# 44 instead of 70 small zero products at the start, a planner whose engines begin later, halved first units and new ranks in an attention and channel-mixing kernel

## The chip, the cores and the metric

The kernel runs on one core of one Trainium2 chip. The metric is the time of one execution on the device in microseconds (us); less is better. A profile is one execution taken by the hardware profiler. Engines are written as in the profile: PE is TensorE's matmul stream and PEld its weight loads, DVE is VectorE, ACT is ScalarE, POOL is GpSimd, SP is SyncE, whose queue starts the DMA transfers.

## What is computed

Three layers follow each other, on a batch of 4 with 576 positions. In the reference, shortened:

```python
# attention: 8 heads of 64; heads 0-3 look back 32 positions, heads 4-7 look back 32 steps of 4
scores = np.where(mask, 1/np.sqrt(64) * q @ k.T, -1e9)
x = softmax(scores) @ v                    # heads joined: (4, 576, 512)
# mixing with the position before
xk = mu_k * x + (1 - mu_k) * x_prev;  xr = mu_r * x + (1 - mu_r) * x_prev
y = sigmoid(xr @ w_r) * (np.maximum(xk @ w_k, 0)**2 @ w_v)
# low rank token mixing and a channel MLP
u = y + ((y.T @ U) @ V).T
out = u + np.maximum(u @ w_ch1, 0) @ w_ch2
```

Weights and activations are kept as float32, and most products run as three matmuls of a high and a low part. The big weights arrive as 64-bit words that DVE and ACT put together into float32 in the kernel.

## The kernel before

**Staging.** The 2304 positions are eight chunks of 288. Attention runs in *units* (one pair of heads, one part of one batch entry): the first four units one by one (`attend`), all later ones two at a time (`attend2`). A unit is: scores on PE (40 small matmuls, L850), masked and negated scores with their least value on DVE (`low`, L775), exponentials with their sums on ACT (`exp`, L784), the reciprocal of the sums (`inv`, L789 and L790), a scaling (`norm`, L801), transposes on PE (L881), a copy from PSUM on ACT (L497), the product with v on PE (L893), and a copy into x. After that come d (the difference to the position before, POOL) and the two mixtures xr, xk (DVE, L1022).

Chunk 0 of the second layer runs in plain float32: first the four rows of w_r (L1081), then eight rows of w_k and eight of w_v (L1096). Its weights come through four buffers of 512 KB (`w64`, loads at L517): ACT and DVE make each into float32 with L535, L536, L540 and L541 (later with L545 and L546). Chunks 1 to 7 use the three-matmul form (L1068 to L1070), with the weights split into wh and wl from 60 us on. Then a transition of about 36 us makes u (L1194 to L1237), and the last half of the kernel is the channel MLP in Strassen-like blocks (L1345 to L1347, L1432 to L1434).

**Order.** Each step is one entry (`op`) of a list: an engine, a guessed duration, a function that issues the instructions, what it reads and writes. `plan` (L253) walks through that list in model time, once: each engine has a time from which it is free (L321, all 0.0), and picks, among the next 160 operations in program order, by `rank` the first that is ready; the ranks are one number for each of the 3453 operations, packed in a string (`RANKED`). The model has a transfer rate for the loads (L99, L410), a model of PE's instruction memory (L329 to L350: instructions are fetched in blocks of 256, `CODE`, and a block is asked for in advance), and `fill` (L352): where PE would wait over 350 ns it puts in matmuls of zeros, 80% of the gap, at 453 ps a column, and at twice that before `FILL_COLD`. What comes out of `plan` is only an order for each engine and the number of zero products; the waits between engines are set by the real data that the instructions touch, not by the list's entries.

The zero products of `fill` are 128x512 (L1671). Ahead of the first operation of PE, `SMALL` = 70 products of 32 columns (L1668) are issued, as soon as DVE has cleared the tile `zero` (L1662).

Of the kernel before, what the change touches and what calls it, by code (L numbers as in the profile page):

```python
# [22 lines left out]
P = 128  # L23
# [17 lines left out]
def unit_kind(pair, part):  # L41
# [51 lines left out]
FILL, FILL_FROM, FILL_NS, FILL_COLD = 0.8, 350.0, 0.453, 5300.0  # L93
# [5 lines left out]
RATE, RATE_TILL, RATE_LATER = 340.0, 40000.0, 290.0  # L99
# [3 lines left out]
SMALL, SMALL_AT = 70, 3500.0  # L103
# [4 lines left out]
    'c-k$S1(a1)7su~=lMF)*oic<-Bhp9+NJ&UYBPD!DcZZZnNJxitBi)jsgn){GAV^BbFboVZ_1^t{fA@Q9optX$XZNXn_CC)Ea-1}d<7}aP>$>hVo*z?w2'  # L108
    'z8v?FI@LJ&y#VkyVmcz$>|-ZK5f4PH<)q(+~49|cbM04&Lp|+9iFel9VZiQ1Av=ETNCi}zH;4%;Qt1G8DK`yb{m+n)FtwKFU57AB)e{0q~lZs=Y|J9@a'
    '!DrI6qN;ANY3QW%9Z1yWm_%<v0Vuc?#TR2wV+zoC%a!VUAN<vVdC#*<yi><yj5bQk2#AU3YyB#~Bmjy7RL-j^r-<&~>w9<M|po&`o*cx|?{uedf9~Gda'  # L110
    '$@=dRlj9lU8Br(CS-&OnFBz=no6PSXU}-H*(X@GAh!Hf%8ZrR#nN-zo6T1&<Zr-v{>|I*f;IL0~hWa|-ayX-f-!A9Ngu-5#LBJZP>5w-_*ocz#6PTi%;'
    'N6BS%UcV|Fr0Ju+)e>rkY0B1A!Pm#S4-w*iS0p4`#Iv`UC$~)NVK4mL5>V}Mu!HvhBPiSk7e1++wr@#+FmQL{P3hYLBHH7aiN*?O{$odjtvH|xEFh%IA'
    '`M|A#Ry*X`6v23a=5}<uOI-tCSMt7wy3di>1I|~xx1ufvdOriRi~3#AxryBS;PXASFC+Uyl>H4^&(gm?0oUuX>v}Vwx9kYdYsj|M=bBL{U!ud7r`R8x5'
    '5^9spizMKnlxtt{~Pcyzf&F=OCrY^40(y~ztF!W?dNzO1MDEaA0ppv`0k<ZI7owdPZKN!&>7mtkgGQ|mI510-9_vj3XP?dy1YMSe8eGZcKFvtpE&d?9I'
    ')rV;0ypRHQ!e$3$Virz6<b-2L1+g8&iK88WYno4tQ=xo`11radZra)@*F;FgG4DMl%AtGQHXJH6p4%WXp-jF%r51v26=*Mxpn=(5IW-naMUkHMR!xJWP'
    '8H+QtCCf#(p~*QR!y9ssw)wwd665WEG{%>lL&Jg!g%)7}|AQRui7n+)WA0`R+m$;6^^5F2Y=j)z`#>KbN5ANW0jPZge*nNJ7McMm-OM%M?xoPf_-XuPI'
    'w0k(>x{X4#+Bm+1(r6Vv+X)lTlmw10eT?@)sO037`^>12dkf$<r&nPdb_d%<W#ydD;p!YuYCn)XtzK4trfEfzi|7m@L=Rs`#4Bc+h2ia(A!aHg@v!KJ$'
    ';8djU51-k0D0Rmu^}%aHo7SeG$WVfIy2IItEXA2WHKEy;G4(!eH{eqY+;+6@1wIq+ccJkGYeYETb17+o$%hR~Q(u+(J=m!!^EZh;?}5zE>E8{Ei|dTb;'
    '?OLQetTf}T4Mmboyc<px*sBk*4<DPsGuo>ESnie|3a?~vbBL$W_V<#Z3Hw%%2wdchfYP>n=yW#BKst0RfBFi=0tI5m4R*vY?(&u7Vq&I7nFGLzosq$T_'
# [84 lines left out]
def tile_attention_mix_channel(  # L204
# [48 lines left out]
    def plan():  # L253
# [61 lines left out]
        def forward(rank):  # L315
# [36 lines left out]
            def fill(o, t):  # L352
# [1412 lines left out]
```

## Time and profile before

| | us |
|---|---|
| median of 3 timed runs | 723.0 |
| lowest and highest | 722.59 and 724.48 |
| the profiled execution, its time | 726.78 |
| the profiled execution, its span from the first to the last instruction | 725.0 |

The profiled execution is 3.78 us above the median of the timed runs, and 1.78 us of its time lie outside the span. All positions below are us from the span's start. Busy time of a matmul is modelled, so a busy PE may still be working at its lower clock, or on zeros; the views by line tell the zeros (L1668, L1671) from real work.

### The profile page before, as it was taken

The numbers are of one execution on the slowest core, as the hardware profiler recorded it, in microseconds if no ns is written. First come the engines' busy times: TensorE is split into PE (matmuls) and PEld (weight loads), VectorE is DVE, ScalarE is ACT, GpSimd is POOL, SyncE is SP. The second block draws the span as 40 slices with busy tenths as digits, with TensorE's granted clock in tenths as the row PEclk, the third lists the DMA queues.
The fourth block names the chain that finished last, engine by engine and source line by source line (L and its number), as shares of the span: only waits on it lengthen the run. The fifth ranks groups of instructions, "written<-read, shape, count | busy, mean of one in ns | idle before, by whom it ended". The sixth has DMA issues, their size and how long they took to land.

```text
span 725.0 us, 19194 instructions
## 1 busy us (share of the span) xinstructions
PE 715.4 (99%) x7542; PEld 690.8 (95%) x7542; DVE 599.4 (83%) x1525; ACT 422.2 (58%) x1049; POOL 129.5 (18%) x164
## 2 busy tenths in 40 slices
PE   9998999999999999999999999999999999999997
PEld 7776999999999999999799999999999999999997
DVE  5886987898777634889998999999998898897763
ACT  5996795868586745365643544455674545454331
POOL 0111265646473634130000000000000000000000
PEclk9998999999999999999999999999999999999999
DMA  9986347787746530746645446353553223030212
GB/s 321 343 291 201 103 170 226 254 270 253 237 146 245 183 96 27 250 154 201 204 124 193 143 159 212 108 184 104 184 183 91 60 71 105 30 118 31 88 48 84
DMA packets 69963, 117.71 MB, mean 162 GB/s; under 512 B 6128, under 2 KB 41200, under 8 KB 69872
## 3 DMA queue, kind: packets, MB, share of 16 engines
q1 hardware_dynamic: 69872, 116.49, 48.9%
q8 instruction: 59, 0.97, 0.6%
q14 instruction: 32, 0.26, 0.1%
HBM read 85.00 MB, written 31.46 MB: 161 GB/s over the span
## 4 chain that ended last, share of the span: by engine, by line
PE 91%; DVE 5%; issue 1%; ACT 1%; DMA 1%; DVEq 0%; ACTq 0%
PE psM L1068 10%; PE psM L1070 10%; PE psM L1069 9%; PE psM L1345 8%; PE psM L1346 8%; PE psM L1347 8%; PE psM L1096 5%; PE psS L1434 4%; PE psS L1432 4%; PE psS L1433 4%; PE psM L1434 4%; PE psM L1432 4%; PE psM L1433 4%; PE psS L985 2%; PE psS L929 2%
## 5 line engine op out<-in xcount | busy, mean ns | idle before, releaser
L1068 PE MATMUL psM<-xk,wh 128*128 128x288 f32 x336 | 101.0, 301 | 0.0
L1070 PE MATMUL psM<-xk,wh 128*128 128x288 f32 x336 | 99.5, 296 | 0.0
L1069 PE MATMUL psM<-xk,wl 128*128 128x288 f32 x336 | 98.1, 292 | 0.0
L1068 PE MATMUL psM<-k2s,wh 128*128 128x288 f32 x224 | 67.4, 301 | 0.0
L1070 PE MATMUL psM<-k2s,wh 128*128 128x288 f32 x224 | 66.3, 296 | 0.0
L1069 PE MATMUL psM<-k2s,wl 128*128 128x288 f32 x224 | 65.5, 292 | 0.0
L1069 PEld LDWEIGHTS psM<-xk,wl 128*128 128x128 f32 x336 | 63.9, 190 | 0.2
L1068 PEld LDWEIGHTS psM<-xk,wh 128*128 128x128 f32 x336 | 63.1, 188 | 0.8
L1070 PEld LDWEIGHTS psM<-xk,wh 128*128 128x128 f32 x336 | 63.0, 188 | 0.0
L1345 PE MATMUL psM<-boxraw,wh 128*128 128x256 f32 x198 | 55.7, 281 | 0.0
L1347 PE MATMUL psM<-boxraw,wh 128*128 128x256 f32 x198 | 55.5, 281 | 0.0
L1346 PE MATMUL psM<-boxraw,wl 128*128 128x256 f32 x198 | 55.5, 280 | 0.0
L492 POOL TENSOR_TENSOR k2s<-k,k2s 128x288 fp32r<-128x288 f32 x49 | 44.0, 904 | 60.7 <-ACT k2s L497 59.7
L1434 PE MATMUL psS<-boxx,wh 128*128 128x256 f32 x192 | 53.9, 281 | 0.0
L1345 PE MATMUL psM<-boxw,wh 128*128 128x256 f32 x186 | 53.1, 286 | 0.1
L1347 PE MATMUL psM<-boxw,wh 128*128 128x256 f32 x186 | 52.2, 281 | 0.0
L1346 PE MATMUL psM<-boxw,wl 128*128 128x256 f32 x186 | 52.2, 281 | 0.0
L784 ACT ACTIVATE pr<-pr,mn 128x64 f32<-128x64 f32 x144 | 48.1, 336 | 1.8 <-DVE mn L775 1.7
L492 POOL TENSOR_TENSOR xk<-m,xk 128x288 fp32r<-128x288 f32 x48 | 44.1, 927 | 26.5 <-ACT xk L497 24.3
L497 ACT ACTIVATE boxx<-ha 128x512 fp32r<-128x512 f32 x32 | 20.1, 628 | 42.4 <-DVE ha L653 38.8
L1069 PEld LDWEIGHTS psM<-k2s,wl 128*128 128x128 f32 x224 | 42.6, 190 | 0.1
L1068 PEld LDWEIGHTS psM<-k2s,wh 128*128 128x128 f32 x224 | 42.1, 188 | 0.5
(236 smaller groups left out, 2495.9 us busy)
## 6 DMA issues: line engine op xcount, KB each, us to landing
w<-w2raw SPq DMA_DIRECT2D x32, 512.0 KB, 4.7
w<-w1raw SPq DMA_DIRECT2D x20, 512.0 KB, 6.5
w2f<-w SPq DMA_DIRECT2D x32, 256.0 KB, 2.6
ub<-uf SPq DMA_DIRECT2D x32, 256.0 KB, 3.0
ws<-w2f SPq DMA_DIRECT2D x24, 256.0 KB, 4.0
raw<-qk SPq DMA_DIRECT2D x16, 320.0 KB, 6.3
ytmp<-y SPq DMA_DIRECT2D x32, 144.0 KB, 3.0
yb<-ytmp SPq DMA_DIRECT2D x4, 1152.0 KB, 7.7
```

The costliest lines, as they stand in the source:

```text
L492: op("POOL", t, lambda: nc.gpsimd.tensor_tensor(out=out_(), in0=a(), in1=b(), op=ALU.subtract), r, w, 40, lock=True)
L784: nc.scalar.activation(pr[:, d : d + KW], pr[:, d : d + KW], AF.Exp, bias=mn[:, i : i + 1], scale=-1.0, accum_out=sm[:, i : i + 1])
L1068: nc.tensor.matmul(a, lhsT=wh, rhs=xh, start=start, stop=False)
L1069: nc.tensor.matmul(a, lhsT=wl, rhs=xh, start=False, stop=False)
L1070: nc.tensor.matmul(a, lhsT=wh, rhs=xl, start=False, stop=stop)
L1096: pe(2, MM1, lambda o=o, acc=accs[o]: nc.tensor.matmul(acc()[:, :HS], lhsT=whole_w[w]()[:, o * P : (o + 1) * P], rhs=cols(src, n), start=f ...
L1345: nc.tensor.matmul(a, lhsT=wh(*wi), rhs=xh(*ci), start=start and n == 1, stop=False, skip_group_check=True)
L1346: nc.tensor.matmul(a, lhsT=wl(*wi), rhs=xh(*ci), start=False, stop=False, skip_group_check=True)
L1347: nc.tensor.matmul(a, lhsT=wh(*wi), rhs=xl(*ci), start=False, stop=last, skip_group_check=True)
L1432: nc.tensor.matmul(a, lhsT=wh(*wi), rhs=xh(), start=start, stop=False, skip_group_check=True)
L1433: nc.tensor.matmul(a, lhsT=wl(*wi), rhs=xh(), start=False, stop=False, skip_group_check=True)
L1434: nc.tensor.matmul(a, lhsT=wh(*wi), rhs=xl(), start=False, stop=stop, skip_group_check=True)
```

## The change

`SMALL` falls from 70 to 44. The planner's engines begin at times of their own (`STARTS`: PE 3.85 us, DVE 1.4, ACT 2.01, POOL 0.9, SP 0.74) in place of 0. The rule that counted the first gap of PE from `SMALL_AT` is dropped, since PE now begins there. `FILL_COLD` goes from 5.3 to 8.0 us, so zero products planned before 8.0 us count twice their time. The planner's transfer rate has three stages in place of two. For units 0 to 3 the entry of the six `low` and that of the five `exp` become two entries each (two score groups, then three), so the list has 3461 entries; the instructions are the same. All ranks are new numbers.

```diff
@@ -90,114 +90,113 @@
 SLACK_PE = 100.0
 
 LATE = 1500.0
-FILL, FILL_FROM, FILL_NS, FILL_COLD = 0.8, 350.0, 0.453, 5300.0
+FILL, FILL_FROM, FILL_NS, FILL_COLD = 0.8, 350.0, 0.453, 8000.0
 PLAN_PRINT = None
 NORM_ENG = ("DVE", "DVE", "ACT", "DVE", "POOL")
 MIX_ENG = ("POOL", "POOL")
 XK_ENG = "DVE"
 TURN = 70.0
-RATE, RATE_TILL, RATE_LATER = 340.0, 40000.0, 290.0
+RATE_FIRST, FIRST_TILL, RATE, RATE_TILL, RATE_LATER = 260.0, 2700.0, 345.0, 36000.0, 290.0
+HALVED = 4
 
 
 CODE_ASK, CODE_END, CODE, CODE_PACE = 140, 449, 256, 60.0
-SMALL, SMALL_AT = 70, 3500.0
+SMALL, SMALL_AT = 44, 3850.0
+STARTS = {"PE": SMALL_AT, "DVE": 1400.0, "ACT": 2010.0, "POOL": 900.0, "SP": 740.0}
 CODE_NS, CODE_BUSY, CODE_GO = 5000.0, 6500.0, 1300.0
 
 
 RANKED = (
...
 )
-RANKS = [50 * x for x in itertools.accumulate(struct.unpack("<3453i", zlib.decompress(base64.b85decode(RANKED))))]
+RANKS = [50 * x for x in itertools.accumulate(struct.unpack("<3461i", zlib.decompress(base64.b85decode(RANKED))))]
 
 
 @with_exitstack
@@ -318,7 +317,7 @@
                 o.done = o.before = None
                 for x in o.tiles:
                     x.end = None
-            free = dict.fromkeys(("PE", "DVE", "ACT", "POOL", "SP"), 0.0)
+            free = dict(STARTS)
             held = {"DVE": 0.0, "POOL": 0.0}
             queues = {e: [o for o in ops if o.eng == e] for e in free}
             mode = {"PE": None, "ACT": "exp"}
@@ -362,9 +361,7 @@
                     since = max((d.done for d in o.bank_deps), default=0.0)
                 room = t - max(free["PE"], since)
                 if x is None or room <= FILL_FROM:
-                    return None, 0, 0, True
-                if SMALL and not begun > 2 * SMALL:
-                    room = max(0.0, t - SMALL_AT)
+                    return x, 0, 0, True
                 pace = FILL_NS * (2 if t < FILL_COLD else 1)
                 return x, wide, int(FILL * room / (pace * wide)), new
 
@@ -407,7 +404,7 @@
                 queues[e].remove(o)
                 if e == "SP":
                     begin = max(t + 1300, dma)
-                    dma = begin + o.size / (RATE if t < RATE_TILL else RATE_LATER)
+                    dma = begin + o.size / (RATE_FIRST if t < FIRST_TILL else RATE if t < RATE_TILL else RATE_LATER)
                     o.done = dma + 700
                 else:
                     o.done = t + o.ns + o.more
@@ -870,17 +867,39 @@
             norm(eng, pr(), 4 * KW, sm(), 4, 1, 5 * KW)
             norm(eng, pr(), 0, sm(), 0, 5)
 
-        op("DVE", 190 + 6 * LOW, lows, [(x,) for x in sc] + [("cst",)], [(pr,), (mn,)], 60)
-        op("ACT", 5 * EXP, exps, [(pr,), (mn,)], [(pr,), (sm,)], 190, mode="exp")
-        op("DVE", 305, lambda: inv(sm(), 5), [(sm,)], [(sm,)], 80, lock=True)
-        normed(u, 6, 2, norms, [(pr,), (sm,)], [(pr,)])
+        if u < HALVED:
+            def lows_of(some):
+                for i, (e, c, d, m) in enumerate(slots):
+                    if i in some:
+                        low(sc[e](), c, pr(), d, m, mn(), i)
+                for e in range(2):
+                    if 4 in some:
+                        low(sc[e](), 2 * KW, pr(), 4 * KW, mk[2], mn(), 4, head(e))
+
+            def exps_of(some):
+                for i in some:
+                    exp(pr(), i * KW, mn(), sm(), i)
+
+            for h, some in enumerate(((0, 1), (2, 3, 4))):
+                op("DVE", 190 + (len(some) + h) * LOW, lambda some=some: lows_of(some),
+                   [(x,) for x in sc] + [("cst",)], [(pr, h), (mn, h)], 60)
+            for h, some in enumerate(((0, 1), (2, 3, 4))):
+                op("ACT", len(some) * EXP, lambda some=some: exps_of(some),
+                   [(pr, h), (mn, h)], [(pr, h), (sm, h)], 190, mode="exp")
+            ks = [(sm, 0), (sm, 1)]
+        else:
+            op("DVE", 190 + 6 * LOW, lows, [(x,) for x in sc] + [("cst",)], [(pr, 0), (pr, 1), (mn,)], 60)
+            op("ACT", 5 * EXP, exps, [(pr, 0), (pr, 1), (mn,)], [(pr, 0), (pr, 1), (sm,)], 190, mode="exp")
+            ks = [(sm,)]
+        op("DVE", 305, lambda: inv(sm(), 5), ks, ks, 80, lock=True)
+        normed(u, 6, 2, norms, [(pr, 0), (pr, 1)] + ks, [(pr, 0), (pr, 1)])
         yield
 
         def tr():
             for i in range(3):
                 nc.tensor.transpose(pt()[:, i * P : (i + 1) * P], pr()[:, i * P : (i + 1) * P], ident)
 
-        pe(3, 3 * 108, tr, [(pr,), ("cst",)], [(pt,)], "tr")
+        pe(3, 3 * 108, tr, [(pr, 0), (pr, 1), ("cst",)], [(pt,)], "tr")
         yield
         copy(3 * P, lambda: pts()[:, : 3 * P], lambda: pt()[:, : 3 * P], [(pt,)], [(pts, 0)], psum=True)
         yield
```

## Rows read from the trace of the kernel before

**Rows 1.** Page, part 1: busy time, share of the span and instructions.

```profile
PE 715.4 (99%) x7542; PEld 690.8 (95%) x7542; DVE 599.4 (83%) x1525; ACT 422.2 (58%) x1049; POOL 129.5 (18%) x164
```

**Rows 2.** Busy time by stretch: stretch, length, busy (instructions) of engines, clock, DMA.

```profile
core 0: us, PE busy (x) PEld busy (x) DVE busy (x) ACT busy (x) POOL busy (x), PEclk, DMA share, GB/s
9.21:18.44 9.23, 8.97 (x220) 6.78 (x221) 7.96 (x53) 7.47 (x32) 0.75 (x1) 1.00 1.04 384
18.44:31.43 12.99, 12.54 (x187) 9.50 (x183) 11.46 (x40) 11.18 (x32) 2.47 (x3) 1.00 0.98 323
31.43:54.73 23.30, 23.23 (x335) 17.99 (x335) 19.80 (x61) 21.57 (x69) 1.84 (x3) 1.00 0.88 314
54.73:56.77 2.04, 0.00 (x0) 0.00 (x0) 0.00 (x0) 1.94 (x4) 0.84 (x2) 0.83 0.99 317
56.07:62.90 6.83, 6.13 (x31) 4.39 (x32) 5.26 (x32) 4.03 (x9) 1.16 (x2) 0.50 0.70 245
60.00:319.90 259.90, 259.90 (x3367) 252.36 (x3366) 197.87 (x605) 176.96 (x514) 118.56 (x146) 0.99 0.57 190
319.90:356.30 36.40, 35.07 (x243) 31.80 (x241) 35.92 (x77) 20.68 (x44) 4.24 (x5) 1.00 0.54 180
```

**Rows 3.** Chain of work that ended last, first 60 us: start, us, what.

```profile
1.45 3.91 PE psM L1668 x70
5.36 0.83 PE psM L850 x40
6.20 3.01 PE psM L1671 x8
...
9.80 1.14 PE psM L1671 x4
...
21.65 6.83 DMA w<-w1raw
...
54.73 2.04 issue
```

**Rows 4.** Busy time by stretch of the zero products of L1671 (PE, PEld).

```profile
6.20:9.21 3.01, 3.01 (x8) 2.12 (x8) 1.00 1.01 379
9.21:18.44 9.23, 4.30 (x14) 2.32 (x14) 1.00 1.04 384
319.90:356.30 36.40, 3.18 (x12) 2.18 (x12) 1.00 0.54 180
```

**Rows 5.** Timeline: start, us, engine, line, operation.

```profile
0.74 0.40 SPq L764 DMA_DIRECT2D raw<-qk  x1
2.61 0.44 SPq L764 DMA_DIRECT2D raw<-qk  x1
9.96 0.08 DVE L775 DVE_READ_ACCUMULATOR2_ANT mn<- 128x1 f32 x1
10.09 0.35 ACT L784 ACTIVATE pr<-pr,mn 128x64 f32<-128x64 f32 x1 [0.44 <-DVE mn L775]
10.79 0.08 DVE L775 DVE_READ_ACCUMULATOR2_ANT mn<- 64x1 f32 x1
10.90 0.17 DVE L789 TENSOR_SCALAR sm<-sm 128x5 f32<-128x5 f32 x1
```

**Rows 6.** DMA issues of 0:1 us, then of 2.5:3 us, with us to landing.

```profile
raw<-qk SPq DMA_DIRECT2D x1, 320.0 KB, 3.4
...
raw<-qk SPq DMA_DIRECT2D x1, 320.0 KB, 5.5
```

**Rows 7.** Page, part 3: instruction fetches; then the DMA view of 54:56 us.

```profile
q8 instruction: 59, 0.97, 0.6%
...
q8 instruction: 1, 0.02, 3.4%
```

**Rows 8.** Busy time by stretch of L1096 alone, at two granted clocks.

```profile
58.00:62.00 4.00, 4.00 (x10) 2.85 (x9) 0.50 0.73 270
64.00:68.00 4.00, 4.00 (x18) 3.11 (x18) 1.00 0.54 208
```

More of the change, by code (lines that the diff above doesn't have):

```diff
@@ new lines @@
+    'c-l3a1-z9-6Nle(&Mmr>5JXA@6u5vQ(jg6kqI5|}qkbSFozmT*fP%Cr0*VNd0@5O#($anVyx;R@*85}GeP?%PXJ>2bWRLQ^RG#O}B@GYz{xR}Wq`Qf}z'
+    'k&Q7=`B*S@B10}Z+Fo1szrES8DP^$Zvsyh@Vx7!M@havn*4KMrKx+K^dspKc>9q)r+*i|??-yx_q6G7+xJ^Bcr(&=;NOzglK%DWZymUT;EZR?8;tn_uz'
+    '2X|1AIw}@Bc>IY{064w;}bHXt$2`^{CHGc`$9~Fm7SS^Pc+tmNewlwIG{E|Hbs%81lSweD9?E5qZ0S@gYBaIRb18?Ml(+0kAJg!)Vi-JP7PN^8S2B3MX'
+    'kK<yO!WLBFDmUp?OUM?%*&%JZPB0(9(n;`^FMnbe-QRCF@V);Qm<5A0yH=j{XMIpG9HabVxmCIqY=<#D8Qe4nKLD0KY=-j~E5;0u6(+E*G!n;QWCfX11'
+    'Oc|M)z<#_D-AJTp-WA%&iycg*|fxcntlgP{SJ%ajv<f-VF8$A0N_a*Yb$d`hD8+aR1E>C$k@XNFt1f8Fe=LJ^fzVA09Uk0A-wA;-b|DoMu@jC%tGQTzn'
@@ new lines @@
+    'HcwDJo5y9^eMg(7l;0swLq$9Cn&ju9r3?8E+DuL{zSY$}(H=~;@4p$lhV}vNj?s>P{=1a30%Mw9QBp0pZ|7>g;rAit`zmnl#hIiqsVw~(FvhKborjC0>'
+    'cFm(Vo6>3{))Qe^esT1kMCv-a1lOh@1LXZ4BFLzfEQTvBeW|A92R(!L<4C&bwz167<hxQtyL4s%QSaV95iZ=F(vN=X)rhn(&jesp3r`S@=AEu`jPK11M'
+    'wTQsYvS0K5xf5W~023{vU%gg1*z~cO2MsQZM=zBu@ku53W3#BeXOZf9d}-XJZ-gSZMDKj%5&+iSi2C?V-&-tXn$jd-C0u?;*^+Bsc@~9j&thd?@`6ksq'
+    'dh1Gs;JhHd0oq3u5K7f1tvO#^Rs+I&h~d2qJmTkBRI*vqu}n3R*W5a15lp8~!arktexC$yUhd_TGNS+vdrd0OfY0ozRb(zNYPstt}~y0=JuX}6y_d_%c'
+    '~_(}dXZ8`w&3%)MUQHk;<U~f^r4!*A38NHa>1KPespXWkG+hD#2@ZFvKJ?#r}%{QL@P59oIV*4x3v-RiGuTI@x<Zo-=kaTzbu6+S46Zs$F1^8bD?_;$m'
@@ new lines @@
+    'WfslQvK4r5z6<FRrhY3~0a9<~`cBC1fOI<NtVJDonTB=;fX~q0V}EXE&*TO^g!)R9#{sM0**;$iyaD}(FwX+q4b#$ckFxe<*$+eE*D>mI3Ky`Sbg$E{4'
+    ')Deiw)cza{op$bbbYUR(Pj#C7lWt&lF9;KMS7R=dEhIU=Sc9ihsN95XQUee<HbCk9o@y$CsDo%t{&PG(3i*U#Sq`as9Q|AKlM3uCq&r(9tAyxfQuIm`K'
+    '}F~vA}AiXU)hf)9*OxC^Q!#&ju}9pd%OGGvJNxf!4sI!S@?DhA{3Nx84WX@54EFL*Y+#`griFB5fl`T(90(y@$}Id-^){vw;_3-v8>nhinfGrOia(J-~'
+    'Z}{50bnrfqt?VYJCizM66SfhPt0PpJPJ*zthv<!Rt5O*ueb4BT%~H<A82k4O2=56;&qKc>u*_&b>MO7N8fcQoaD;7d*2P`*=x|6A60AMGkYPaN}aPWcv'
+    'XGJ+?T^giX0z$fZVkU!Mj#D*SC`yl-%!3&+=8VvS`&Ga$#7j-WA9z@?e&|HD~BOyCGFHqLKH-@^0w95#s&4G=A#^!o|Xp;|E5orAoerE^9(s>6+87Vi`'
@@ new lines @@
+    '#Yn$Sq)R#*y1$r@?&xvg-2zR8nbSqqX$kZ!15a9Tm#1xe+AJk?r~T)&?MQx`{x`_;08a;ODD&zJJxv&U2xmVJx%S9b=02HuX9C|4?KQ~w4p=nvkKwS!G'
+    'Dc0^v%tQk-A}ap61-jE!+YR;gS;s4qu{;(zN*YacU4_?r|Df6of&k$LF+8&ctv*sI6tAhj5FI79Gk)U0rewj-wM17NS^^qL%&Np*UbMIG;gG>_S+<IbR'
+    '_BhZbrLh5~}o$1Diup@=7}JpVgkEJ{$Q$@DI}4&v#Sm+IjZAR+0=t-kG|A+K;5Yz<wspV*F*`obQ=jr?)#%Z>eNQ`1KF`$PZo9$@%oo(soSP?!s3{dRw'
+    '=J?VUYCI?8ut-FM)*7PdD;Z$Js)vq)2by$OB40AC)kw_oq)`(cxX>X28~Jriws&QM>6B-nQlPzzp<h`0B*8*s^{gQ+_SU75&(;Qj~LVaoHMdmnpY75ge'
+    'H`TdOC#mKEOto^It=oq#)RCiSz{r_MM26LfD@qL5#yIJ$TTo8p=kUqdiAtQaFI~Cq`(*7sc8_@#%uhF+Tw4DL=KWML?V)uIqaQs3#L3t~*WswX;-2=W4'
@@ new lines @@
+    'GR{0wFY12-Ut#SV@a%%FJm5<2?it<1_o%xLO?ml#&&f4+lWgrLXdgK_UH9x&@=~;WOnnNtOETVAXxc<M23lj8d#Xr#=l6i89(C7XXqfNr&{2athBMec#'
+    'pKS*dLzMAhW?qu_D<c^`Z1Pd%maKMqTOu0<KR6Aj`YA5F_-M%E=<3-NxG+FVOU{sU1KdWasI{v|6K1N{EfNGS<2;k#i_r4i?@~eW_gag;tujELd7-+=|'
+    '}&u*?H#>PESYMd*4X16pzmW>feW+(|Q|e)9XA(CO3BqG{>Qs^r0>nYrh%1HzjXSu1w)@T9fA`S9|bg4s#zPe$!8HN-5^_EAz_){U<5^&z)bra}D?&1ii'
+    'WwPtjjIUnDt{^6&`b-K)^p3izE!lR+fgX)WtOzuw#a38tUS(z-IneA;~hYy)&;hMuW<+gP_o;G7Q6_CwoR%4K-_a)P_8<Zjxn&A>X|w|74eZT2ze-ta9'
+    'uurkr6(><^A2k&bFdtS1vWG8rEg^Rc>7xpA*dl}j)Q1>TwyMR@`$Gref-P8R!Q#q;69kO|>ksbgYT^RoY-@j`AFoyth_<>w^cR$*U0#_UQ9A=;007pG='
@@ new lines @@
+    '{lXm2hfT*AD|rHVU)qcSN0@ez%((+&y$c_ji*|7RrgJ6Pn=}`ihJm*k`G+CX1&YAuEYLHI`ZdyZ*@Kgr!}6yl=SjACm$q-{{m+ct1bj1ej-*}REZotY^'
+    ';|I~hh>Al7|M5O`xo;Y1zpMT@omX2Q4(l8uN%BMl3-_cAh1T1^~M*VeG==D2Hey64%4qad-nk2{UJRQ{`6-I$<~djp9$}Do^(&QrhH##B4lUvBXC~;zK'
+    'Z!2qW@yxMJ1m@^Sj{uh5EhpY0OwhfZdg>$DAL4e=+arR>>p@ri*L__B-pnn0bB=zK`_&)ApqHDIJf%lex_42j)FM?+as{mY&KQoPf@Dq}PGv*ImJU+kx'
+    '+rWG(K=HIyr`ZY^m066M^fO!hs_xc9W5$)#7FX6z)^b_H$P)Au*ZlkeMo-H`8O;KzYwhxY35ZEuRnib?d>e(4X6GP?Vj>vU*&0&nIpZcEPbZsrgPEgdD'
+    '3NKTPVC>ahuUZsCkXsQ68&XU&#|0DQUQL;Vbo@C5S+%>)7!Lx7O1$z5#**z3X-A~}I7BJh%ThwP`%ma+EhH^FdA#=qJ-COiK#XR(0Yh6dWx4r^=Xvo+d'
@@ new lines @@
+    '=zo%SvfUh!UH~1d;LB9%W`XZp*%ZK0_^Ii?1t`~Hz8NCyEtGv_m-IizT<6}N<GRBo1L|!ey+KL~4Qs%4jdqV{_X_krklxAM+cC!vs5`{^x1uhO<R|KfL'
+    '&tc=tPIW-T1$A^oc`MKU(mK1<2>Y}En}SpPb%hKlf9l5e3#&DXW$*U5G#OdGT$wseX8a}x)o!_j@yzop|3uDssqo*c;mR+Ix}8+`c#H*d06{s+HMAR8a'
+    '}{&|7ZC039uw+%S)Rz^j!}vh2Y73=)XmM9q3Kqjw{Zb)=Sr7UH1d41zk0DHr%@{9a6R~y<LsOZ`okNcHVTJ{?vU#I!wDRjMqYM810{<zERj@!B6>KptA'
+    '+7<!Rg4Gd@XPeot#d-2(cSlCDBZ)_UvCV@_w7ZzjnALA(DdK$PU~9`xJ8d?!*jn7*rl)s-#|kJke~P2T`KuR}SKv%H1<d4zST!n~%yn_jei2z(~|EvkE'
+    'vadq$aB`-nWMzrbA_Yum{3u@C(@3rK;knTNT*Pv;<^mE28&-WSVkp8{{+(iRstB`FjKke^Qt_W;5Z3nWx3&AHlTubSXNv21pz^gd$H<X?lG+l5!_<p3_'
```

144 lines of the change are left out of this document (53 added, 91 removed).

## Prediction

> **What bounds the kernel now.** I read the shares of the engines first. PE is busy for 715.4 of 725.0 us [rows 1], so nothing but work taken off PE, or a better use of its time, can show. Busy is not useful, though, so the second view is the busy time by stretch [rows 2], and beside it the same stretches for the zero products alone [rows 4]. Three stretches differ from the rest. Up to 18.44 us PE is nearly always busy, but 3.01 + 4.30 = 7.31 us of that are zeros (22 products), and 3.91 us more are the 70 small ones [rows 3, 4]. From 54.73 to 56.77 it does nothing, and from 56.07 to 62.90 it runs at a granted clock of 0.50 [rows 2]. From 319.90 to 356.30 DVE is busy for 35.92 of 36.40 us and PE has 3.18 us of zeros and 36.40 - 35.07 = 1.33 us of idling [rows 2, 4]; here DVE sets the pace. Between 60 and 319.90 PE is never idle [rows 2]. So the third view, the chain of waits, is needed for the first 60 us alone [rows 3]: the small zeros, the first scores, the large zeros, one weight load of 6.83 us, and 2.04 us of "issue", in which PE waits for nothing that the profile shows.
>
> What is saved before 60 us therefore reaches 319.90, since PE has no idle time there that could swallow it, provided that DVE and ACT keep up (198 and 177 us busy of 260 [rows 2]). It reaches the end if the DVE stretch, whose work hangs on the last chunk, moves along unchanged.
>
> **Part 1, fewer small products.** 70 take 3.91 us, so one takes 0.056 us, and 44 take 2.46 us: PE is free at 1.45 + 2.46 = 3.91 us in place of 5.36 [rows 3]. The first scores need unit 0's load, issued at 0.74 us and landed 3.4 us later [rows 5, 6], so at about 4.1 us. They start at 4.1 to 4.2: 1.2 us earlier. [...]
>
> **Part 2, the cold price of zeros till 8.0 us.** Between the scores of units 0 and 1 stand 8 large zeros, 3.01 us or 0.376 us each, against 1.14 / 4 = 0.285 us for the next four [rows 3]. [...] They end at 9.21, but unit 1's data was issued at 2.61 and landed 5.5 us later, at 8.1 [rows 5, 6]. Counted at twice the price, half as many products fit a gap, and the scores of unit 1 can start at 8.1 to 8.2: 1.0 us earlier. This is the same microsecond as that of part 1 for later units, not one more.
>
> **Part 3, engines that begin late, rates, new ranks.** No instruction comes or goes; the order changes, in all of the kernel. At the start, the divide of unit 0 (L789) stands at 10.90 us on DVE behind the last score pass of unit 1, which ends at 10.87 [rows 5]; unit 0's five exponentials began on ACT ahead of all this. A plan that knows that unit 1 can't come before 8 us can put the divide first. SP's queue is moved too: the load of 6.83 us on the chain [rows 3] is issued when a weight buffer comes free, and the buffers follow the order of ACT and DVE. How much that gives can't be read from one row. A lower bound is nothing, or a loss, if the ranks put something else in the way. An upper bound comes from ACT, the engine nearest to full beside PE: it idles 9.23 - 7.47 = 1.76 and 12.99 - 11.18 = 1.81 us in the two stretches up to 31.43 [rows 2], and can begin 1.2 us earlier, so the rows of chunk 0 can't start more than 4.8 us earlier. After that ACT is busy 21.57 of 23.30 us and PE 23.23 [rows 2]: no room to gain, little to lose. In the stretch in which DVE sets the pace the new order can win back at most what PE spends on zeros and idling there, 3.18 + 1.33 = 4.5 us [rows 2, 4], and can lose about as much by other DVE work put in between; nothing in the trace leans either way, so I take 0. Of parts 1 to 3 together I take **2.0 us**: 1.0 to 1.2 from earlier scores, and about half of the 1.8 us for which a divide could have stood earlier.
>
> **Part 4, halves.** I price this at nothing. Unit 1's first exponential started at 10.09, when its own minimum was written (9.96 + 0.08), while the score passes went on to 10.87 [rows 5]: the waits already go by data, group by group. Two list entries in place of one only let other work be put in between. If that happens, one exponential is 0.35 us [rows 5], so it is worth a few tenths either way.
>
> **Part 5, the stall.** PE has 7542 + 7542 instructions [rows 1] and its queue fetched 59 blocks [rows 1, 7], 256 instructions each; the kernel's planner models just that (`CODE`). In the 2.04 us in which PE stood still, one such fetch came, with the DMA engines at a share of 0.99 [rows 2, 7]. So I read the stall as PE waiting for code behind data, in a burst of attention (up to 80 matmuls of scores right behind 64 to 80 of the product with v, some 300 instructions). The change drops 26 products, 52 instructions, plus some large zeros, ahead of every later block boundary, and the order of the bursts is new: the old coincidence of burst and boundary goes. Whether another one arises can't be read from before. Bounds: 2.04 us gained if none does, nothing if one like it does. I take the gain, because it is the only hole of this size up to 319.90 [rows 2].
>
> Behind the stall lies a second cost. The clock fell to 0.50 at 56.07, while PE idled, and was back at 62.90 [rows 2]. At 0.50 PE did 10 instructions of L1096 in 4 us, at 1.00 it did 18 [rows 8]. From 56.77 to 62.90 are 6.13 us at half pace: about 3.07 us lost. But the profiled execution is 3.78 us over the median of the timed ones (726.78 and 723.0). That is nearest to this loss, so I assume that the timed executions mostly have no fall and I count none of it; the other end is 3.07 us more.
>
> [...]
>
> **The sum.** Profiled: 726.78 - 2.0 - 2.04 = 722.7 us. Timed, 3.78 us lower: **719.0 us**.
>
> **The rivals.**
> - *The hole stays or moves, or the timed runs never had it.* Only the 2.0 us of the start remain: 721.0 us. For it: the attention bursts are as dense as before and the DMA share is 0.88 to 1.04 up to 54.73 [rows 2]. Against it: no other hole up to 319.90.
> - *The start's gain is swallowed.* The rows of chunk 0 wait for weight loads: the chain goes through one of 6.83 us at a DMA share of 0.98 [rows 2, 3]. If the loads can't come earlier, the scores come earlier for nothing: 723.0 us with a hole, 721.0 without. I count it at 723.0.
> [...]
> - *Slower: two holes in place of one, with the clock falling in the timed runs as well.* [...] Each hole long enough for a fall costs 2.04 + 3.07 = 5.1 us. The median holds, by my count, one hole without a fall (2.0 us). With the start's gain, two holes of which one has its fall give 723.0 - 2.0 - 2.0 + 2.0 + 5.1 = 726.1 us; two falls would give 729.2. It decides when a block lands over 1.3 us (56.07 - 54.73) after PE has run out.
>
> **How the numbers follow.** Forecast (start and hole): chance 0.40, 719.0 us, its own range 715.9 (the fall counted as well) to 720.8. Hole stays: 0.24, 721.0. Swallowed: 0.14, 723.0. Clock: 0.07, 723.3. Slower: 0.15, 726.1. About 0.3%, 2.2 us, is what a measurement of this kernel can tell from no change: bounds at 720.8 and 725.2. Faster takes nearly all of the first case, 0.10 of the second and 0.02 of the others: 0.51. Slower takes the fifth and a little of the third and fourth: 0.18. Same is the rest: 0.31. The range of 8 in 10 goes from 715.5 to 725.5: below lies little, above lies two thirds of the slower case.
>
> **What would show it.** Right: L1668 x44, ending near 3.9; first scores near 4.2; unit 1's scores near 8.2; the first row of w_r (L1081) 2 us or more ahead of the old place; no "issue" of PE over 1 us up to 100 us; granted clock 1.00 throughout; the stretch in which DVE sets the pace still about 36 us. Wrong: the first L1096 no earlier than 31.43 (swallowed); an "issue" of a microsecond or more elsewhere (hole moved); zeros of 0.37 us each after 9 us (clock); a longer DVE stretch after 317 us. The prediction fails most likely on part 5, which rests on one hole in one profiled execution, and on part 3, since all ranks are new and their effect after 60 us can't be seen in the trace of before.

## The result, and the profile after

The changed kernel takes **727.36 us** (median of 6 runs, 726.6 to 728.38) beside 723.33 us of the kernel before in the same runs (722.59 to 724.78): ratio 1.0051, 95% interval 1.004 to 1.0063. The forecast was 719.0 us, 715.5 to 725.5. The profiled execution of after took 728.38 us, its span is 726.6 us. Lines have moved: the small zeros are L1687 (before L1668), the large ones L1690 (L1671), the first scores L847 (L850), the rows of w_r and of chunk 0 L1100 and L1115 (L1081, L1096), the three-matmul rows L1087 to L1089 (L1068 to L1070), the first step of the transition L1213 (L1194), the two MLP layers L1364 to L1366 (L1345 to L1347) and L1451 to L1453 (L1432 to L1434).

Page, part 1, of after, beside [rows 1]:

```profile
PE 716.6 (99%) x7533; PEld 693.5 (95%) x7533; DVE 597.2 (82%) x1525; ACT 424.2 (58%) x1049; POOL 127.9 (18%) x164
```

PE runs 9 matmuls fewer and is busy 1.2 us longer. Timeline of PE in after, five stretches (start, us, engine, line, operation):

```profile
3.91 0.91 PE L847 MATMUL psM<-raw 64*32 64x64 f32 x40
4.75 5.03 PE L1690 MATMUL psM<-zero 128*128 128x512 f32 x12
9.70 0.66 PE L847 MATMUL psM<-raw 64*32 64x64 f32 x40
...
17.64 0.41 PE L1100 MATMUL psM<-xk,wx 128*128 128x288 f32 x1
...
30.52 0.75 PE L1115 MATMUL psM<-xk,wx 128*128 128x288 f32 x2 [0.72 <-ACT sg L494]
...
57.98 3.05 PE L1690 MATMUL psM<-zero 128*128 128x224 f32 x25 [1.24 <-issue]
60.87 0.66 PE L1115 MATMUL psM<-k,wx 128*128 128x288 f32 x2
...
72.49 0.38 PE L1087 MATMUL psM<-xk,wh 128*128 128x288 f32 x1
```

The same of before, first row of w_r and first three-matmul row:

```profile
18.82 0.89 PE L1081 MATMUL psM<-xk,wx 128*128 128x288 f32 x3
...
73.75 0.38 PE L1068 MATMUL psM<-xk,wh 128*128 128x288 f32 x1
```

The first scores come 1.4 us earlier than in [rows 3]; then 12 zeros stand where 8 stood, and unit 1's scores are 0.5 us later. The rows of w_r start 1.2 us earlier (17.64 against 18.82), those of chunk 0 0.9 us earlier (30.52 against 31.43). At 56.7 to 58.0 PE waits for nothing that the profile shows, and 25 zeros follow. Busy time by stretch of after (stretch, length, then PE, PEld, DVE, ACT, POOL with instructions, granted clock, DMA share, GB/s):

```profile
31.40:54.70 23.30, 23.04 (x353) 17.54 (x352) 17.95 (x56) 20.56 (x64) 1.73 (x2) 1.00 0.80 274
54.70:60.00 5.30, 4.06 (x26) 3.29 (x27) 5.07 (x31) 4.94 (x12) 1.59 (x3) 1.00 0.90 273
60.00:73.00 13.00, 13.00 (x65) 10.54 (x64) 10.77 (x26) 9.16 (x32) 1.69 (x2) 1.00 0.62 214
320.00:358.00 38.00, 36.61 (x266) 34.43 (x266) 37.05 (x80) 22.74 (x47) 2.52 (x3) 1.00 0.65 205
384.00:600.00 216.00, 215.44 (x1801) 215.07 (x1800) 200.02 (x416) 111.47 (x220) 0.00 (x0) 1.00 0.42 134
```

The granted clock is 1.00 in all of them; the stretch at 0.50 of [rows 2] is gone. The first three-matmul row starts at 72.49 us, 1.26 us ahead of before (73.75). So what it loses against this profile lies behind it. Lined up matmul by matmul, after is within 1 us of before at 320 us (whose profile had lost its 2.04 and 3.07 us by then), 2.1 us ahead at 358, and then falls back by about 0.2 us on average in every 200 matmuls, to 1.6 us behind at the end. In that last stretch PE is never short of work in before and waits once, for 0.56 us, in after; the matmuls themselves follow each other more slowly. The commonest time from one MLP product to the next is 117 to 118 ns in before and 120 ns in after.

### The profile page after: what moved, and what is told of

It is laid out like the page before. It is cut to its first block, busy times and chain, and to the rows that moved or that the text cites. A ratio compares the mean times of both kernels' runs of the same rounds, so it can differ in the third digit from the quotient of the medians.

```text
span 726.6 us, 19190 instructions
## 1 busy us (share of the span) xinstructions
PE 716.6 (99%) x7533; PEld 693.5 (95%) x7533; DVE 597.2 (82%) x1525; ACT 424.2 (58%) x1049; POOL 127.9 (18%) x164
## 5 line engine op out<-in xcount | busy, mean ns | idle before, releaser
L1087 PE MATMUL psM<-xk,wh 128*128 128x288 f32 x336 | 101.0, 301 | 0.0
L1089 PE MATMUL psM<-xk,wh 128*128 128x288 f32 x336 | 98.9, 294 | 0.0
L1087 PE MATMUL psM<-k2s,wh 128*128 128x288 f32 x224 | 67.3, 301 | 0.0
L1089 PE MATMUL psM<-k2s,wh 128*128 128x288 f32 x224 | 65.9, 294 | 0.0
L1087 PEld LDWEIGHTS psM<-xk,wh 128*128 128x128 f32 x336 | 63.0, 188 | 0.9
L1089 PEld LDWEIGHTS psM<-xk,wh 128*128 128x128 f32 x336 | 63.2, 188 | 0.0
L1364 PE MATMUL psM<-boxraw,wh 128*128 128x256 f32 x198 | 56.2, 284 | 0.0
L1366 PE MATMUL psM<-boxraw,wh 128*128 128x256 f32 x198 | 56.0, 283 | 0.0
L1453 PE MATMUL psS<-boxx,wh 128*128 128x256 f32 x192 | 54.3, 283 | 0.0
L1364 PE MATMUL psM<-boxw,wh 128*128 128x256 f32 x186 | 53.0, 285 | 0.1
L1366 PE MATMUL psM<-boxw,wh 128*128 128x256 f32 x186 | 51.9, 279 | 0.0
L1087 PEld LDWEIGHTS psM<-k2s,wh 128*128 128x128 f32 x224 | 42.0, 188 | 0.4
L1089 PEld LDWEIGHTS psM<-k2s,wh 128*128 128x128 f32 x224 | 42.1, 188 | 0.0
```

What stands on the lines that cost most here:

```text
L1087: nc.tensor.matmul(a, lhsT=wh, rhs=xh, start=start, stop=False)
L1089: nc.tensor.matmul(a, lhsT=wh, rhs=xl, start=False, stop=stop)
L1364: nc.tensor.matmul(a, lhsT=wh(*wi), rhs=xh(*ci), start=start and n == 1, stop=False, skip_group_check=True)
L1366: nc.tensor.matmul(a, lhsT=wh(*wi), rhs=xl(*ci), start=False, stop=last, skip_group_check=True)
L1453: nc.tensor.matmul(a, lhsT=wh(*wi), rhs=xl(), start=False, stop=stop, skip_group_check=True)
```

## The experiments

What differs in an MLP product between the two kernels? Not its instruction, shape or clock. But a tile gets its place in SBUF when it is first used, tag by tag (a *tag* is a group of tiles that share buffers, as `raw`, `x`, `w`), in one pool. New ranks change which tag comes first, and all later tiles of the program stand elsewhere. From the built programs, the first byte of each tag in a partition:

```
tag   before   after
x       5024   25504
raw    23520    5024
sm    behind w 70720
w      70720   70816      (all weight tiles 96 bytes on)
w64, pr, mn, d, B, A ...  as before
```

*Theory P (places)*: the moved tiles make the products slower. *Theory O (order)*: the new order itself loses the time, through waits. *Theory F*: part 5 of the prediction, that timed runs mostly have no fall of the clock.

In all that follows the ratio is against runs of the kernel before on the same chip; **pitch** is the mean time from the start of one product to that of the next, worked out from all starts in the trace between 73 and 320 us and from 384 us on, pauses over 200 ns left out.

**First: which of the two, order or places.** The places are set by giving each tag a pool of its own, in a chosen order:

```diff
-    pool = ctx.enter_context(tc.tile_pool(name="pool", bufs=2))
+    pools = {t: ctx.enter_context(tc.tile_pool(name=f"p{t}", bufs=2))
+             for t in "x raw w64 pr mn w w32 sm pt d sig rt B m A y k2 us vs".split()}
...
-            self.args, self.tag, self.bufs, self.home = (shape, dt, name), tag, bufs, home or pool
+            self.args, self.tag, self.bufs, self.home = (shape, dt, name), tag, bufs, home or pools[tag]
```

*The kernel before once more*, with no edit:

> The kernel before, unchanged, with a profile and per-execution clocks. Theory F (the profiled execution on which the prediction rests had a fall of the clock at 56 us that the timed ones mostly don't have): this profile has a granted clock of 1.00 from about 8 us to the end, its span is 721 to 722.5, and the place of the first chunk-1 product (L1068) is about 70.7 us in place of 73.75; the timed clocks are 0.999 or 1.000. Rival (the fall belongs to every execution, the 3.8 us between profiled and timed are the profiler's): span near 725, clock 0.995 again. Ratio 1.000 in both.

Measured: 723.62 us (723.08 to 726.63, 10 runs), ratio 1.000 [0.9985, 1.0015]. The profile came as theory F has it (span 721.9 us, first three-matmul row at 70.70 us, granted clock 1.00 at 54 to 64 us); the timed clocks did not, as shown further down.

*The changed kernel at the old places*, the edit above:

> The changed kernel, with every tile tag in a pool of its own so that all tiles lie at the SBUF addresses that they had before; order of work as changed. Theory P (places): the matmuls of the last half took 120 ns from start to start in the changed kernel's profile where 117 to 118 stood before, because the new ranks change which tags are first used and so where the tiles lie; with the old places that comes back: about 2.3 us less than the changed kernel, 724.5 to 725.5, ratio to before 1.002 to 1.003. Theory O (the order of the products and their neighbours sets the pitch): 727.4, ratio 1.005 to 1.006.

Measured: 723.9 us (722.42 to 726.77, 12 runs), ratio 0.9992 [0.9975, 1.0009]. All of the loss is gone, more than I had expected.

*The kernel before at the new places*, the same edit in before with the tags in after's order ("raw x w64 pr mn sm w w32 ..."):

> The kernel before with its own order, but every tile at the address that it has in the changed kernel. Theory P: the pitch of the last half goes from 117.5 to 119 to 120 ns; 725 to 726, ratio 1.002 to 1.004. Theory O: 723.3, ratio 1.000.

Measured: 728.33 us (725.83 to 729.76, 6 runs), ratio 1.0061 [1.0039, 1.0083]. The old order loses as much as the changed kernel as soon as its tiles stand where the change puts them. That is more than the 725 to 726 us expected. Theory P holds, O falls. The stretch in which PE is full tells it in one number, the matmuls done. The kernel before again, busy time by stretch:

```profile
384.00:600.00 216.00, 216.00 (x1821) 215.78 (x1820) 200.55 (x417) 111.23 (x219) 0.00 (x0) 1.00 0.45 139
```

The kernel before at the new places:

```profile
384.00:600.00 216.00, 216.00 (x1810) 215.81 (x1809) 199.68 (x416) 110.34 (x217) 0.00 (x0) 1.00 0.45 139
```

The changed kernel at the old places (at its own, above, it did 1801):

```profile
384.00:600.00 216.00, 216.00 (x1820) 215.73 (x1819) 202.23 (x420) 112.98 (x222) 0.00 (x0) 1.00 0.43 134
```

*The changed kernel without the 25 zeros at 58 us:*

```diff
+            if o.eng == "PE" and wide == CW - HS and many == 25:
+                many = 0
             for _ in range(many):
```

> The changed kernel without the 25 zero products (128x224) at 57.98 to 60.87 us, ahead of a row of w_v. Theory Z (the zeros, issued late after a wait for code, hold back a product whose weight DVE had ready at 58.8): the product starts near 58.9, 2.0 us earlier, and the time is 1.5 to 2 us less than the changed kernel, 725.4 to 725.9, unless the pause of PE (56.7 to 58.9) lets the clock fall. Rival W (the weight or something else comes last): the product stays at 60.5 or later and the time at 727.4. Rival C: the clock falls and the time rises by up to 3 us to 729 or more.

Measured: 727.13 us (726.15 to 727.93, 10 runs), ratio 1.0038 [1.0024, 1.0052]. Little is won. What PE waits for there without the zeros (waits of PE: line <- releaser, us in total, times, longest):

```profile
PE psM L1115 <- DVE wx L543: 2.1, 1, 2.1
```

Its busy time by stretch:

```profile
54.70:60.00 5.30, 3.22 (x11) 2.13 (x10) 4.96 (x23) 4.96 (x16) 1.60 (x3) 0.86 0.90 290
60.00:73.00 13.00, 13.00 (x58) 10.39 (x58) 11.27 (x26) 9.46 (x30) 1.82 (x2) 0.93 0.56 197
```

The zeros fill a real wait for a weight that DVE has not made yet, behind 12 score passes that the new order puts ahead of it (54.58 to 57.2 us in after). This run's profile shows that wait; how much of it each other execution has is not shown. Without them PE idles 2.1 us and the granted clock falls there to a mean of 0.86 and 0.93. The first three-matmul row starts at 71.51 us in place of 72.49.

**Second: which place.** The changed kernel again, with one move at a time. *Theory W*: the weights must start at a multiple of 64 bytes. *X*: the swap of x and raw costs. *D*: it is the distance between the moving tile and the weights.

*Weights 96 bytes on, x and raw at the old places* (tags "x raw w64 pr mn sm w w32 ..."):

> The changed kernel with only the weight tiles (tags w and w32) at their new place, 96 bytes on (first w tile at 70816 of each partition, a multiple of 32 but not of 64); x and raw stand where the kernel before had them. Theory W (the start of the weight tiles decides: a product whose weights do not start at a multiple of 64 bytes loads and runs 1 to 4 ns later): the whole loss of about 4 us is here, 727 to 728 us, and L1088's products of rows come every 133.5 ns, not every 129.5. Theory X (the swap of x and raw decides): 723.9 us as with the old places, L1088 at 129.5 ns. Theory D (it is the distance between the moving and the weight tile, so any move of either costs): 725 to 728 us.

Measured: 724.22 us (722.42 to 727.11), ratio 1.0007 [0.9993, 1.0021].

*x and raw swapped, weights at the old place* ("raw x w64 pr mn w w32 sm ..."):

> The changed kernel with only x and raw at their new places (raw from 5024, x from 25504); the weight tiles start at 70720 as in the kernel before, a multiple of 64. Theory W: no loss, 723.9 us, L1088 every 129.5 ns. Theory X: 727 to 728 us, L1088 every 133.5 ns (its moving tile lies in x). Theory D: 725 to 728 us.

Measured: 725.36 us (723.91 to 726.71), ratio 1.0011 [0.9996, 1.0026].

*Weights 128 bytes on* (a pad of 128 bytes ahead of w in the old order of tags):

> The changed kernel with x and raw at the old places and the weight tiles, and all that lies behind them, 128 bytes on (first at 70848, a multiple of 64 again): 128 bytes of padding stand ahead of them. Theory W (multiples of 64): no loss, 723.9 us, L1088 every 129.5 ns. Theory X: no loss either. Theory D: 725 to 728 us. With f1 it tells whether a move of the weights costs in itself or only to a start between multiples of 64.

Measured: 721.65 us (720.04 to 724.54), ratio 0.997 [0.9953, 0.9988].

*Weights 96 bytes back* ("x raw w64 pr w w32 mn sm ..."):

> The changed kernel with x and raw at the old places and the weight tiles 96 bytes back (first at 70624, a multiple of 32 and not of 64; the small mn tiles stand behind them). Theory W: the loss is there again, 727 to 728 us, L1088 every 133.5 ns. Theory X: 723.9 us. Theory D: 725 to 728 us.

Measured: 722.97 us (721.38 to 725.99), ratio 0.9992 [0.9975, 1.0009].

W falls: weights at a start of 32 modulo 64 cost 0.0015 of the 0.0059 between after and its old places when they are 96 on, and nothing when they are 96 back. X falls: the swap alone costs 0.0019, a third. D as put here, that any move costs (725 to 728 us in each run), misses three of the four as well: 724.22, 721.65 and 722.97 us. No single move makes the loss; the two together do, and cost more than their sum (by the pitches below 4.6 us beside 1.0 and 1.8). Sums of the three products' pitches in ns; price = the differences to before at 560, 512 and 512 products for each line, in us:

```
kernel                          L1087-9  L1364-6  L1451-3  price  ratio
before again                      396.8    354.6    356.2    0.0  1.0000
before, new places                399.4    356.4    358.6   +3.7  1.0061
after                             399.5    357.9    358.9   +4.6  1.0051
after, old places                 396.9    354.8    356.4   +0.3  0.9992
after, weights 96 on              399.4    353.2    356.7   +1.0  1.0007
after, x and raw swapped          396.8    357.5    356.9   +1.8  1.0011
after, weights 128 on             396.7    350.9    355.0   -2.6  0.9970
after, weights 96 back            396.8    356.2    353.0   -0.8  0.9992
after, 64 apart (below)           396.8    351.6    353.9   -2.7  0.9971
before, 64 apart (below)          396.8    351.5    353.9   -2.8  0.9964
```

A ratio of 0.001 is 0.7 us, so price and time agree to about 1 us in each line, which is what the intervals allow. For a second form of D, made after these four runs, each product of six traces (before, after, the four above) was matched to the addresses of its two tiles. Mean pitch by the distance of their starts, modulo 128 (number of products; pauses over 150 ns left out):

```
distance         0             32            64            96
L1364-1366   119.3 (1952)  117.8 (2509)  117.1 (3216)  119.5 (556)
L1451-1453   119.0 (3299)  118.9 (1600)  117.1 (1020)  118.9 (2691)
```

64 apart is the best of both layers; in the second the other three are equal. In after 448 of the 512 products of each of the second layer's first two lines are 0 apart and none 64; in before 112 are 0, 304 are 96 and 16 are 64 apart. In the first layer after has 264 of 512 at 0, before none. With the means of the table these counts explain about 0.9 of the 1.7 us that after loses in the first layer and 0.1 of the 1.4 in the second. The rest is open: at 0 apart the second layer's products took 119.4 ns in after and 118.8 in before. In the rows (L1087 to L1089) there is no exception: all products are 0 apart in the kernels with 399.4 ns and more, 64 or 96 apart in those with 396.7 to 396.9, which is 1.5 us.

**Third: a forecast by D, and the parts of the change at good places.** The tags in the order "raw w64 x pr w w32 mn sm pt d sig rt B m A y k2 us vs" put 384 of 512 products of each line of the first layer and 352 of 512 of the second's first two lines 64 apart.

*The changed kernel 64 apart:*

> The changed kernel with the tags laid out so that in most products the moving tile and the weights start 64 bytes apart, modulo 128: order raw, w64, x, pr, w, w32, mn, sm and so on (weights from 70624, raw from 5024, w64 from 25504, x from 41888). Of the 512 products of each line of the first layer 384 are 64 apart and 128 are 0 apart (changed kernel: 248 and 264); of the second layer's first two lines 352 of 512 are 64 apart (changed kernel: none, 448 are 0 apart). Theory D (the distance decides; 0 apart costs 119.2 to 119.6 ns, 64 apart 116 to 117.2 ns in the runs so far): the sum of the first layer's three lines falls to 350 to 352 ns (changed kernel 357.9), that of the second layer's to about 353 ns (358.8), and the time to 720 to 721 us, below both kernels. Theory R (each place has a price of its own that no distance tells): anything between 722 and 727 us, with sums of 354 ns and more.

Measured: 722.26 us (719.81 to 724.31, 12 runs), ratio 0.9971 [0.9953, 0.9988]. The sums are 351.6 and 353.9 ns, where D forecast 350 to 352 and about 353; 1830 matmuls from 384 to 600 us in place of 1801:

```profile
384.00:600.00 216.00, 216.00 (x1830) 215.64 (x1829) 203.07 (x423) 113.97 (x225) 0.00 (x0) 1.00 0.43 136
```

The time missed the forecast by 1.3 us or more. A wait that no profile of the old order has can be part of it: PE in the transition, for a load of yb, and a fall of the granted clock behind it. Waits of PE:

```profile
PE psS L1213 <- DMA yb<-ytmp: 2.0, 1, 2.0
```

Busy time by stretch:

```profile
350.00:356.00 6.00, 4.55 (x14) 3.70 (x15) 3.73 (x9) 3.31 (x7) 0.00 (x0) 0.55 0.59 190
```

Such a fall was seen in the new order alone: seven of its ten profiles have one between 348 and 361 us (mean granted clock 0.80 to 0.90 from 345 to 362 us), none of the four of the old order has (1.00). Two of those four have theirs at the hole of 56 us instead, and of the new order's only the two that left PE idle there for over 2 us. What a fall at 350 us costs, no run isolates.

*The same with 6 zeros between units 0 and 1*, which part 2 of the prediction had counted on (`if o.eng == "PE" and many == 12: many = 6`, ahead of the same loop):

> As the kernel 64 apart, with 6 wide zero products in place of 12 between unit 0's scores and unit 1's: the count that my part 2 had forecast. It tells what the misread of the cold price cost. Theory C (carried): unit 1's scores begin at 8.6 to 8.8 us in place of 9.7, and the end comes 0.8 to 1.0 us sooner than in the kernel 64 apart. Theory S (swallowed, because the clock rises later with fewer products or because the stretch of VectorE at 320 to 358 us ends when it did): scores at 8.6 to 8.8 us or later, the end within 0.3 us of the kernel 64 apart.

Measured: 720.97 us (719.02 to 725.29, 12 runs), ratio 0.9949 [0.9932, 0.9966]: faster than both kernels. The start, on PE's timeline:

```profile
4.00 0.90 PE L847 MATMUL psM<-raw 64*32 64x64 f32 x40
4.84 2.92 PE L1692 MATMUL psM<-zero 128*128 128x512 f32 x6
8.13 0.66 PE L847 MATMUL psM<-raw 64*32 64x64 f32 x40 [0.37 <-DMA raw<-qk]
```

Unit 1's scores start at 8.13 us, sooner than expected here and as the prediction had it, now waiting 0.37 us for their data. The end comes 0.0022 (1.6 us) sooner than with 12; the intervals of both overlap, so carried is likelier than swallowed and not certain.

*The kernel before 64 apart:*

> The kernel before, with its own order of the work, its 70 small products and whole units, laid out as in the kernel 64 apart. It tells what the change's order is worth once both have the same good places. If the order is worth the 1.3 us by which the two profiled spans at the old places differ (721.9 and 720.6): 721.7 to 722 us here against 720 to 721 us in the new order. If the order is worth nothing: equal within 0.5 us. In both cases below the kernel before by 2.5 to 3.5 us if theory D holds.

Measured: 721.39 us (719.27 to 723.55, 12 runs), ratio 0.9964 [0.9948, 0.998]. Against 0.9971 of the new order at the same places: the order is worth nothing that these runs can tell.

*The changed kernel 64 apart with 70 small products* (`small = 70`, the order as planned for 44):

> As the kernel 64 apart, but with 70 small zero products ahead of the first scores in place of 44; the order is left as planned for 44. It undoes part 1 alone. Theory C (the lead of the start is carried to the end): first scores at 5.2 to 5.4 us in place of 3.9, the end 1.3 to 1.5 us later. Theory S (swallowed): first scores as late, the end within 0.3 us of the kernel 64 apart.

Measured: 725.72 us (722.75 to 728.35, 12 runs), ratio 1.0013 [0.9994, 1.0032]: 0.0042 or 3.0 us worse than with 44, more than twice the 1.36 us by which the first scores are later (5.30 against 3.94). Both theories miss. The waits of PE show what else came:

```profile
PE psS L948 <- issue: 2.1, 1, 2.1
PE psM L1088 <- issue: 1.7, 2, 1.0
...
PE psS L1213 <- DMA yb<-ytmp: 0.6, 1, 0.6
```

The 26 products more shift every later instruction of PE, and with 64 apart and 44 no "issue" of this size stood anywhere. So the run doesn't price part 1 by itself. The mean granted clock, listed with each timed run, was 0.997 or less in 10 of these 12 runs, in 8 of 12 with 44.

## Why the prediction was wrong, point by point

In short: by itself the new order is worth about nothing, and a side effect of it, tiles at other places in SBUF, makes PE's products slower, by some 4.3 us in all.

- **The step that failed: part 3, "No instruction comes or goes; the order changes, in all of the kernel."** It priced new ranks as order alone and so put the places of the tiles at nothing. They also set the first use of each tag and with it the place of every tile. The places cost +4.6 us by the pitches; giving them back takes 1.0051 to 0.9992, 4.3 us, and giving them to the old order costs 1.0061. No rival held this: the range's upper part was there for holes and falls of the clock. Nothing in the trace of before shows a place, but the code does: one pool, and a tile made on first use.
- **Its order, alone, was forecast 4.0 us better (719.0 against 723.0)** and is 0.0008 better at the old places, -0.6 us [-1.8, +0.7], or 0.0007 worse at the good ones. Forecast and measured change are 8.0 us apart: about 4.3 are the places, about 3.4 this gain that didn't come. It went as follows.
- **Part 1 was right in its step**: first scores at 3.91 us, forecast 4.1 to 4.2. Its worth at the end could not be isolated: undoing it costs 3.0 us, but moves holes as well.
- **Part 2 read the rule wrongly.** I took double price for the gap ahead of unit 1. `pace` looks at the time of the operation *behind* the gap: 12 products at 0.232 us are 80% of at least 3.48 us, and from 4.75 us that is 8.2, later than `FILL_COLD`. So the single price was used, more zeros came in place of fewer, and they ran at 0.42 us each (5.03 / 12). With 6 the scores start at 8.13, within the 8.1 to 8.2 of the prediction: the mechanism was right, the count was not worked out through the code. In every trace the zeros come every 427 ns ahead of the first record of the granted clock and about every 231 ns behind it (the record starts at 8.28 us in before, inside the eight zeros and not behind them, and at 9.09 in after). The 1.00 of [rows 4] doesn't tell the clock there, since the views print 1.00 for the time ahead of that record. That PE was at a lower clock in the zeros of 427 ns is an estimate from these two spacings and from L1096 in before, whose products start every 480 ns while 0.50 is granted and every 243 ns at 1.00.
- **The start's 2.0 us** were 1.2 at 17.64 us and 0.9 at 30.52. They were eaten at 57 to 61, where the order makes DVE late with a weight and PE fills the time with zeros: at the old places the first three-matmul row starts at 70.36 us, in the profile of before again at 70.70:

```profile
70.36 0.37 PE L1087 MATMUL psM<-xk,wh 128*128 128x288 f32 x1
...
70.70 0.38 PE L1068 MATMUL psM<-xk,wh 128*128 128x288 f32 x1
```

  That is the rival "swallowed", by DVE and not, as I had it, by weight loads.
- **The stretch of DVE, taken at 0**: in the profiles at the old places the new order wins 1.6 us there (last L1213 at 357.42 against 359.36 in before again, with a lead of 0.34 ahead of it), within the bounds of 4.5. Six zeros fewer, at 3.18 / 12 = 0.265 us each [rows 4], are as much. A wait ahead of L1213 that no profile of the old order has, of 0.6 to 2.3 us in six of the new order's (five times for the load of yb), gives part of it back.
- **Part 4, halves at nothing**: not tried by itself; the divide of unit 0 stands at 7.33 us in place of 10.90 [rows 5], as part 3 had hoped.
- **Part 5, the stall**: half right. The same program shows it at another size in each execution: before 2.04 us in the first profile [rows 3] and 1.43 in the next (below); in the old order at other places 0.34 and 1.50. The new order's profiles with 44 small products have 1.24 (after), 0.97 (weights 128 on) and, in the others with zeros there, 0.24 us or less. So by these few profiles the change took most of a hole of about 1.3 us, not one of 2.04. That PE waits for code there was not tried, but fits the traces: all profiles together have seven "issue" waits of PE of 0.9 us or more, and in each of them one fetch of instructions had landed 1.2 to 1.5 us before PE went on (in before at 55.33 us, PE at 56.77; in after at 56.48 and 57.98). That data held up the fetch, no trace shows: it took 1.09 us in before, and all 59 of that trace took 0.88 to 1.76 us. Waits of PE in the kernel before again:

```profile
PE psS L929 <- issue: 1.4, 1, 1.4
```

  and in after, where it stands ahead of the 25 zeros:

```profile
PE psM L1690 <- issue: 1.2, 1, 1.2
```

- **The clock, theory F**: wrong as a statement. Of the 29 runs of before beside the first four kernels, 13 had a mean granted clock of 0.997 or less, and these took 724.16 to 727.43 us; the 16 at 0.998 and more took 722.42 to 725.52. The median lies between. Part of the timed runs has the fall, so it could have been counted in part. Nor does a hole of over 1.3 us decide it: the profile with 1.43 us kept its clock at 1.00, the one with 1.50 lost it (mean 0.83 from 54 to 64 us).
- **The rivals**: "Clock" (0.07, 723.3 us) counts 2.3 us for real work that is slower up to 18.44 us, and no run shows that term. What the profiles show is zeros every 427 ns up to the first record of the clock and every 231 ns behind it, as above; this record starts at 6.3 to 9.2 us in the nine profiles with 44 small products and at 8.3 to 10.6 us in the four of the old order. 12 zeros took 5.03 us in after's profile and 3.85 us in the same order at the old places. "Two holes", the slower one, gave nearly the right time (726.1) by a mechanism that was not there: after's six runs have a mean clock of 0.997 to 1.0.

That the places make the loss is shown; that it is the distance is not. *Why* 64 bytes should help is open, and the rule isn't the whole of it. In the first layer 64 and 32 apart took 117.4 and 118.1 ns in before, but 116.0 and 117.2 ns with the weights 128 on, where every distance modulo 128 is the same: the gain of that run, 0.9970, comes from no distance in the table. Its first layer, with a quarter of the products 64 apart, is faster (350.9) than that of "weights 96 on", with all of them (353.2). And in the rows 64 and 96 apart are equal.

## What to carry to other kernels

An edit that only reorders a program can still move its tiles: compare the addresses of the built programs before explaining a slow drift by order, and pin the places (a pool for each tag, in a fixed order) before comparing two orders. Where PE is full, compare the pitch of equal products in both traces first; a drift without waits is seen there, in no wait and no chain. And a constant in a planner is worth what the code makes of it: put the numbers through the rule that uses it.

## What the runs showed of the hardware that was not expected

The pitch of equal products at granted clock 1.00 goes with the places of the tiles in SBUF: over six programs 117.1 ns on average when moving tile and weights start 64 bytes apart modulo 128, 119.0 to 119.3 ns when 0 apart, with exceptions as above. For some 4,750 products other places made ratios of 1.0061 and 0.9964 to before (728.33 and 721.39 us) out of one and the same order. A weight tile that starts off a multiple of 64 bytes didn't in itself cost anything measurable (1.0007 and 0.9992).

Near the start of every profile equal zeros come every 427 ns and later about every 231 ns. The clock's first record stands between them, at 6.3 to 10.6 us: at 8.3 and 10.6 us in two executions of the very same program.
